# Where the second batch's k and v are averaged: from TensorE's products to VectorE's reductions

## The chip, the cores and the metric

The kernel runs on one core of a Trainium2 chip. The metric is the device time of one execution in microseconds (us); the figure for a kernel is the median of its runs. Five engines work side by side, each through its own queue in order: TensorE (PE in the profile, its weight loads PEld), VectorE (DVE), ScalarE (ACT), GpSimd (POOL) and SyncE (SP), which here issues most DMAs. TensorE writes into PSUM, from where ScalarE and VectorE read.

## The reference, cut to what matters

Attention over pooled keys and values, then a dense feed-forward layer, then a layer of eight experts of which each token takes one. All in float32.

```python
# q, k, v: (8, 8, 576, 64) = batch, head, sequence, head_dim
k_p = k.reshape(B, H, Sp, 8, D).mean(axis=3)        # Sp = 72
v_p = v.reshape(B, H, Sp, 8, D).mean(axis=3)
attn = softmax(q @ k_p.T / sqrt(D))
x = (attn @ v_p) -> (4608, 512)
x = relu(x @ w_in) ** 2 @ w_out                      # d_ff = 2048
out = top-1 of 8 experts: gate * (relu(x @ w1[e]) @ w2[e])
```

The change concerns the first two lines for the second of the eight batches: sums over groups of eight neighbouring rows of k and v.

## The kernel before, in words

The 4608 tokens are 18 tiles of 256: for each batch two "reg" tiles of its first 512 tokens, and after every fourth batch a tile of what is left over. A float32 product is made of three products of split operands (a high part rounded for TensorE, a low part with the rest). One tile against one of eight chunks of the first layer's weights is a step of `Stream.step` (line 352): twelve products for layer 1 (line 285), then ReLU and square on ScalarE and GpSimd (`act_square_first`, line 300), and two steps later six products for layer 2 (`pop`, lines 361 and 336).

The attention of a tile is computed during the tile before it, as small jobs put by hand between those steps. `at(ti, pos, f)` (line 664) files job `f` under tile `ti` and one of 16 positions, two for each chunk; `run_jobs` runs what is filed. The order in which jobs are issued is the order on each engine's queue.

**The first phase.** Tiles 0 and 1 (the first batch) run together, their sixteen steps interleaved by `order` (line 961): tile 0's chunk c sorted at 2c, tile 1's at 2c + 5. Loop index `i` from 0 to 7 runs the jobs filed under tile 0, `i` from 8 to 15 those under tile 1. In the same phase the weights arrive as float64 and have to be converted: `first_steps` (line 250) yields 80 steps, ten for each chunk. Five VectorE instructions join the two 32-bit halves of one half chunk (lines 216 to 229), then ScalarE casts the high part (`wh_m`, line 264) and GpSimd subtracts the low part (`wl_m`, line 265). `conv(n)` issues n such steps. From `i` = 2 to 12 three steps are issued beside a step's layer 1 (`beside`) and three after its layer 2 (`after`), 25 having been issued before. Layer 1 of chunk c needs the first half of its weights, layer 2 the second.

**k and v of a batch.** `pool_load` (line 406) brings k or v into three buffers: two of 128 partitions by 2 x 512 and a third with the rows left over. Each partition holds eight rows of 64 side by side, for one or two heads. `pool_first` (line 437) sums the eight rows of a piece. With a `bank` it lets TensorE add eight products with the identity into a PSUM buffer (lines 448 and 449); with `None` it calls `pool_reduce` (line 433), one VectorE reduction (line 435) that writes into a tile kept in SBUF. Then ScalarE copies the sums twice, each time through a mask that leaves one of the two heads (line 463, tiles `km`, `vb` and `vr`); k's third piece is only copied (line 453, tile `kr`), which a reduction makes unnecessary, as it writes there itself. Batches 2 to 7 use `pool_reduce` and GpSimd.

**The second batch.** Its jobs stand in the first phase. The three pieces of k go to positions 6, 7 and 8 of tile 0 (`plan_k`, list `k` of `FIRST`), which is `i` = 3 and 4; the three of v to positions 0, 1 and 5 of tile 1 (`plan_v`, list `v`), which is `i` = 8, 8 and 10. Around them stands the attention of tile 2 (`plan_reg`, list `tile2`), under tile 1:

- position 0 and 1: the query transposes of the second and the first half (`q_T`, PSUM buffers emptied by ScalarE, line 533), then at position 1 `make_kT`, two groups of transposes of k (lines 489 and 492) that ScalarE copies out (490, 493);
- position 2: scores of the first half and their extremes on VectorE (`scores_first`, lines 561 and 565);
- position 3: the exponentials, eight pairs of ScalarE instructions (line 574);
- position 6: ScalarE's and GpSimd's split of v (`make_vsplit`), normalisation (lines 587 to 595), scores of the second half;
- positions 8 to 15: exponentials and normalisation of the second half, transposes of both (`p_T`, lines 608 and 611), the products with v (`av`, line 624).

All these transposes, scores and sums take turns in one PSUM pool of two buffers, `ps_t` with the tag "tp". A tile that wants a buffer waits until the one before last has been read. `plan_v` files its jobs before `plan_reg` does, so at a shared position v's come first. From tile 2 on tiles run one after the other (line 983). After all 18, the expert phase begins.

Of the kernel before, what the change touches and what calls it, by code (L numbers as in the profile page):

```python
# [25 lines left out]
FIRST = dict(  # L26
    pre=[3, 1, 1, 2, 3, 3], att=[2, 2, 3, 3, 2, 0],
    beside=[0, 0, 3, 3, 3, 3, 3, 3, 3, 3, 3, 3, 3, 0, 0, 0],
    after=[0, 0, 3, 3, 3, 3, 3, 3, 3, 3, 3, 3, 3, 0, 0, 0],
    lag=5, late=11, av=2, spill=[11, 2],  # L30
    k=[6, 7, 8, 11], v=[0, 1, 5, 6, 6], tile2=[1, 0, 1, 2, 3, 6, 6, 8, 9, 10, 13, 15, 15],
    low_dve=[0, 0, 0, 0, 0, 0, 0, 0], bias=[0, 1, 1], vlow_dve=0)


# [8 lines left out]
def moe_pipeline_kernel(  # L43
# [40 lines left out]
    ps_h = ctx.enter_context(tc.tile_pool(name="ps_h", bufs=2, space=bass.MemoryType.PSUM))  # L84
    ps_y = ctx.enter_context(tc.tile_pool(name="ps_y", bufs=2, space=bass.MemoryType.PSUM))
    ps_t = ctx.enter_context(tc.tile_pool(name="ps_t", bufs=2, space=bass.MemoryType.PSUM))
# [319 lines left out]
    def pool_load(src, b, nm):  # L406


        rows = src[b].rearrange("h (a r) d -> (h a) (r d)", r=8).rearrange("(c p) f -> p c f", p=144)
        raws = []  # L410
        for i in range(3):
            raw = akv.tile([P, 2, 512], F32, tag="kvraw", name=f"{nm}raw_{b}_{i}")
            if i < 2:
                nc.sync.dma_start(raw, rows[0:P, 2 * i:2 * i + 2, :])
            elif nm == "k":
                for c in range(4):
                    nc.sync.dma_start(raw[16 * c:16 * c + 16, 0, :], rows[P:144, c, :])
            else:
                pairs = rows[P:144].rearrange("p (g q) f -> p q g f", q=2)
                for j in range(6):  # L420
                    nc.sync.dma_start(raw[16 * j:16 * j + 16], pairs[:, j % 2])
            raws.append(raw)
        return raws

    def pool_dst(nm, b, raws, i):
        if i < 2:
            dst = (kp_t if nm == "k" else vp_t)[b % 2]
            return raws[i], dst[:, 2 * i:2 * i + 2, :]
        if nm == "k":
            return raws[2][:64, 0:1, :], kr_t[b % 2][:, 1:2, :]  # L430
        return raws[2][:96], vr_t[b % 2]

    def pool_reduce(nm, b, raws, i):
        src, dst = pool_dst(nm, b, raws, i)
        nc.vector.tensor_reduce(dst, src.rearrange("p c (r d) -> p c d r", r=8), AX.X, ALU.add)

    def pool_first(nm, b, raws, i, bank):


        src, sums = pool_dst(nm, b, raws, i)  # L440
        n, nc_ = src.shape[0], src.shape[1]
        if bank is None:
            pool_reduce(nm, b, raws, i)
        else:
            src = src.rearrange("p c (r d) -> p c r d", r=8)
            pool, tag, width = bank
            pb_ = pool.tile([P, width], F32, tag=tag, name=f"{nm}sum_{b}_{i}")[:n, 0:nc_ * D]
            for r in range(8):
                nc.tensor.matmul(pb_, ident[:n, :n], src[:, :, r, :], start=r == 0, stop=r == 7)
            sums = pb_.rearrange("p (c d) -> p c d", c=nc_)  # L450
        if nm == "k" and i == 2:
            if bank is not None:
                nc.scalar.copy(kr_t[b % 2][:, 1:2, :], sums)
            return
        if i == 2:
            dst, ms = batch[b].setdefault("vr", a1.tile([96, 2, 2, D], F32, tag="vr", name=f"vr_{b}")), rmask
        else:
            what = "km" if nm == "k" else "vb"
            if what not in batch[b]:
                batch[b][what] = a1.tile([P, 4, 2, D], F32, tag=what, name=f"{what}_{b}")  # L460
            dst, ms = batch[b][what][:, 2 * i:2 * i + 2], mask
        for t in range(2):
            nc.scalar.activation(dst[:, :, t, :], sums, AF.Copy, scale=ms[:n, t:t + 1])
# [14 lines left out]
    def make_km(b, cs=slice(0, 4)):  # L478
        if "km" not in batch[b]:
            batch[b]["km"] = a1.tile([P, 4, 2, D], F32, tag="km", name=f"km_{b}")  # L480
        by_head(batch[b]["km"], kp_t[b % 2], cs)
# [14 lines left out]
    def make_vb(b):  # L496
        if "vb" not in batch[b]:
            batch[b]["vb"] = a1.tile([P, 4, 2, D], F32, tag="vb", name=f"vb_{b}")
            by_head(batch[b]["vb"], vp_t[b % 2], slice(0, 4))
        vr = a1.tile([96, 2, 2, D], F32, tag="vr", name=f"vr_{b}")  # L500
        nc.gpsimd.tensor_tensor(vr, vr_t[b % 2].unsqueeze(2).to_broadcast([96, 2, 2, D]),
                                rmask.unsqueeze(1).unsqueeze(3).to_broadcast([96, 2, 2, D]), ALU.mult)
        batch[b]["vr"] = vr

    def make_vsplit(b, dve, low=True):

        vb, vr = batch[b]["vb"], batch[b]["vr"]
        vh = a3.tile([P, 4, P], F32R, tag="vh", name=f"vh_{b}")
        nc.scalar.copy(vh, vb.rearrange("p c t d -> p c (t d)"))
        nc.scalar.copy(vrem_t[b % 2][:, :, :, D:P], vr)  # L510
        batch[b]["vh"], batch[b]["vrem"] = vh, vrem_t[b % 2]
        if low:
            make_vlow(b, nc.vector if dve else nc.gpsimd)
# [135 lines left out]
        return xh, xl  # L649

    batch = [dict(b=b) for b in range(B)]
    tp_bank, h_bank = (ps_t, "tp", 512), (ps_h, "h", 256)
    xts = {}

    def spill_x(ti):
# [8 lines left out]
    def at(ti, pos, f):  # L664
        jobs.setdefault((ti, pos), []).append(f)

    def plan_k(b):
        m = tiles.index(("reg", b, 0)) - 2
        loc = {}

        def load():
            loc["k"] = pool_load(k, b, "k")
        if b > 1:
            at(m - 1, 13, load)
        else:
            loads[f"k{b}"] = load
        for i in range(3):
            if b < 2:
                at(m, FIRST["k"][i], lambda i=i: pool_first("k", b, loc["k"], i, tp_bank))
            else:  # L680
                at(m, i, lambda i=i: pool_reduce("k", b, loc["k"], i))
        if b > 1:
            at(m, 3, lambda: make_km(b))

    def plan_v(b):
        n = tiles.index(("reg", b, 0))
        loc = {}

        def load():
            loc["v"] = pool_load(v, b, "v")  # L690
        if b > 1:
            at(n - 2, 4, load)
        else:
            loads[f"v{b}"] = load
        for i in range(3):
            if b > 1:
                at(n - 2, (12, 14, 15)[i], lambda i=i: pool_reduce("v", b, loc["v"], i))
            else:
                at(n - 1, FIRST["v"][i], lambda i=i: pool_first("v", b, loc["v"], i, tp_bank))

        tail = tiles[n - 1][0] == "reg" and b % 2 == 0 and b > 0
        if b > 1:
            at(n - 1, 8 if tail else 4, lambda: make_vb(b))
        at(n - 1, 10 if tail else 6 if b > 1 else FIRST["v"][4], lambda: make_vsplit(b, tail))
# [100 lines left out]
    for b in range(B):  # L805
        if b % 2 == 1:
            plan_tail(b - 1)
        if b:
            plan_k(b)
            plan_v(b)  # L810
        plan_reg(b, 0)
        plan_reg(b, 1)
# [232 lines left out]
    def route(ti, ys, yp):  # L1045
        yr = pb2.tile([P, 2, DM + 2], F32, tag="yr", bufs=3, name=f"yr_{ti}")
        lg = pb2.tile([P, 2, NE], F32, tag="lg", name=f"lg_{ti}")
        for u in range(2):
            nc.vector.tensor_tensor(yr[:, u, 0:DM], ys[u], yp[:, u, :], ALU.add)

        def logit(u, e):
            junk = pbr.tile([P, DM], F32, tag="junk", name=f"junk_{ti}_{u}_{e}")
            nc.vector.tensor_tensor_reduce(  # L1053
                out=junk, in0=yr[:, u, 0:DM], in1=wgb[:, e, :], scale=1.0, scalar=0.0,
                op0=ALU.mult, op1=ALU.add, accum_out=lg[:, u, e:e + 1])
        for u in range(2):
            for e in range(NE):
                queue.append(lambda u=u, e=e: logit(u, e))
        st = {}
        fs = [lambda: route_rank(ti, yr, lg, st), None, None, None, lambda: route_count(ti, st),  # L1060
              lambda: route_place(ti, yr, st), None, None, lambda: route_scatter(0, st),
              lambda: route_store(ti, yr), *[None] * SCATTER_GAP, lambda: route_scatter(1, st)]
        if ti == TA:
            fs += after_a()
        if ti == NT - 1:
            fs += after_b()
        queue.append(lambda: chain(fs))
# [402 lines left out]
    for i_, (what, g) in enumerate(items):  # L1470
# [7 lines left out]
        i, c = divmod(g, NCH)  # L1478
# [4 lines left out]
        if g < N1:  # L1483
            x = xb[i]
            stream.step(wch_b[c], x, act_square_b, c, state, f"b{i}_{c}",
                        lambda ys, i=i: route(i, ys, ypb[i]), side)
# [44 lines left out]
```

## Time and profile before

| | |
|---|---|
| median of 3 runs | 1552.11 us (1548.74 to 1552.5) |
| the profiled execution | 1552.05 us |
| its span, first to last instruction | 1550.2 us |
| TensorE busy | 1502.2 us (97%) |
| TensorE's weight loads busy | 1355.9 us (87%) |
| VectorE busy | 1115.5 us (72%) |
| ScalarE busy | 677.5 us (44%) |
| GpSimd busy | 417.2 us (27%) |
| mean granted TensorE clock | 0.979 of full speed |

Times inside the profile count from the first instruction. "Busy" leaves out waits. The time of a group is the sum of its instructions; "idle before" is the time for which the engine had stood still when an instruction began, with the instruction of another engine that ended the wait behind an arrow. Products on TensorE overlap, so their recorded times add up to more than the time that passes. A float32 product with the identity has two records.

### The profile page before, as it was taken

How to read it: one execution, taken by the hardware profiler on the slowest of the kernel's cores; microseconds unless marked ns; L12 is line 12 of the kernel's file. 1: busy time of each engine (PE TensorE's matmuls, PEld its weight loads, DVE VectorE, ACT ScalarE, POOL GpSimd, SP SyncE). 2: the span in 40 equal slices, each digit the busy share in tenths (PEclk: the TensorE clock that was granted, in tenths of full speed). 3: DMA queues.
4: the chain of work that ended last, by engine and by line, in shares of the span. 5: the costliest groups of instructions: out<-in, count | busy, mean ns of one | idle time of the engine just before them, and what ended most of it. 6: DMA issues, size and time to landing. Idle time of an engine off the chain costs nothing. (4 is left out here: it accounts for less than half of the span.)

```text
span 1550.2 us, 27286 instructions
## 1 busy us (share of the span) xinstructions
PE 1502.2 (97%) x9678; PEld 1355.9 (87%) x9678; DVE 1115.5 (72%) x2349; ACT 677.5 (44%) x1422; POOL 417.2 (27%) x506
## 2 busy tenths in 40 slices
PE   6799999999999999999999999999999999999997
PEld 5688889898989999999999999989989888888886
DVE  7776797689867554477777778789866767767763
ACT  4453333233333323444344343355555656665663
POOL 3253335353534434010110111131222221222211
PEclk8699999999999999999999999999999999999999
DMA  9314355446623314655677667599877878888862
GB/s 297 114 56 143 112 167 180 134 159 159 179 86 95 98 57 163 211 96 87 104 98 95 76 103 96 103 213 202 242 256 215 262 255 272 260 265 254 268 226 89
DMA packets 214343, 253.75 MB, mean 164 GB/s; under 512 B 56959, under 2 KB 139007, under 8 KB 214080
## 3 DMA queue, kind: packets, MB, share of 16 engines
q1 hardware_dynamic: 202784, 221.73, 52.3%
q0 software_dynamic: 11424, 30.28, 8.9%
q8 instruction: 76, 1.25, 0.4%
q14 instruction: 59, 0.48, 0.1%
HBM read 198.00 MB, written 55.80 MB: 164 GB/s over the span
## 5 line engine op out<-in xcount | busy, mean ns | idle before, releaser
L1053 DVE CUSTOM_DVE_ANT_0 junk<-yr,wgb 128x512 f32<-128x512 f32 x288 | 198.0, 688 | 4.7
L192 DVE TENSOR_TENSOR wl_s<-raw_s,wh_s 128x1024 fp32r<-128x1024 f32 x144 | 174.8, 1222 | 28.8 <-ACT wh_s L191 26.4
L285 PE MATMUL h_a<-xh,wh_m 128*128 128x256 f32 x576 | 151.2, 294 | 5.2 <-ACT wh_m L264 5.0
L191 ACT CAST wh_s<-raw_s 128x1024 fp32r<-128x1024 f32 x144 | 149.1, 1046 | 10.1 <-DMA raw_s<-in_moe_w_dram 10.1
L285 PE MATMUL h_a<-xl,wh_m 128*128 128x256 f32 x576 | 148.0, 288 | 1.6 <-DVE xl L635 1.6
L316 ACT ACTIVATE r_b<-h_b 128x256 f32<-128x256 f32 x144 | 55.3, 384 | 212.8 <-PE h_b L285 208.9
L285 PE MATMUL h_s<-xh_s,wh_s 128*128 128x256 f32 x576 | 145.6, 286 | 2.2 <-DVE gl_s L326 2.2
L285 PE MATMUL h_b<-xh_b,wh_f 128*128 128x256 f32 x576 | 144.8, 284 | 0.0
L285 PE MATMUL h_b<-xl_b,wh_f 128*128 128x256 f32 x576 | 144.2, 283 | 0.0
L285 PE MATMUL h_s<-xl_s,wh_s 128*128 128x256 f32 x576 | 143.6, 282 | 0.0
L294 ACT ACTIVATE r_a<-h_a 128x256 f32<-128x256 f32 x128 | 49.2, 385 | 212.9 <-PE h_a L285 142.7
L296 POOL TENSOR_TENSOR g_a<-r_a 128x256 f32<-128x256 f32 x128 | 83.0, 648 | 183.3 <-ACT r_a L294 182.9
L1124 POOL DMA_INDIRECT perm_d<-pos,di x36 | 38.2, 1060 | 347.9 <-DVE es L1115 177.8
L319 DVE TENSOR_TENSOR gl_b<-g_b,gh_b 128x256 fp32r<-128x256 f32 x144 | 61.2, 425 | 95.8 <-ACT g_b L318 95.8
L297 POOL TENSOR_TENSOR gl_a<-g_a,gh_a 128x256 fp32r<-128x256 f32 x128 | 96.7, 756 | 102.3 <-DVE gh_a L295 56.5
L336 PE MATMUL y_a<-wh_m,gh_a 128*128 128x512 f32 x288 | 121.7, 423 | 0.0
L285 PEld LDWEIGHTS h_a<-xh,wh_m 128*128 128x128 f32 x576 | 111.9, 194 | 10.1 <-ACT wh_m L264 5.6
L1317 POOL DMA_INDIRECT out_dram<-yo,tidx x36 | 42.0, 1166 | 284.2 <-ACT yo L1314 198.2
L285 PEld LDWEIGHTS h_a<-xl,wh_m 128*128 128x128 f32 x576 | 112.1, 195 | 6.8 <-DVE xl L635 3.3
L336 PE MATMUL y_a<-wl_m,gh_a 128*128 128x512 f32 x288 | 116.5, 405 | 0.0
L285 PEld LDWEIGHTS h_s<-xh_s,wh_s 128*128 128x128 f32 x576 | 108.9, 189 | 8.5 <-DVE gl_s L326 3.7
L336 PE MATMUL y_a<-wh_m,gl_a 128*128 128x512 f32 x288 | 115.9, 402 | 0.0
(322 smaller groups left out, 4144.9 us busy)
## 6 DMA issues: line engine op xcount, KB each, us to landing
raw_s<-in_moe_w_dram SPq DMA_DIRECT2D x288, 256.0 KB, 4.2
raw_h<-in_moe_w_dram SPq DMA_DIRECT2D x112, 256.0 KB, 4.0
y_d<-yr POOLq DMA_DIRECT2D x18, 514.0 KB, 10.2
xs_d<-xh SPq DMA_DIRECT2D x18, 512.0 KB, 2.7
xs_d<-xl SPq DMA_DIRECT2D x18, 512.0 KB, 4.0
yp_d<-ya SPq DMA_DIRECT2D x36, 256.0 KB, 2.1
xh_b<-xs_d SPq DMA_DIRECT2D x18, 512.0 KB, 9.3
xl_b<-xs_d SPq DMA_DIRECT2D x18, 512.0 KB, 11.5
```

The lines of the kernel that those rows point to most:

```text
L191: nc.scalar.copy(wh, raw)
L192: nc.vector.tensor_tensor(wl, raw, wh.bitcast(F32), ALU.subtract)
L285: nc.tensor.matmul(h, w_[:, 0, kk * P:(kk + 1) * P], rhs[:, kk, :], start=n == 0, stop=n == 3 * NK - 1)
L294: nc.scalar.activation(r, h, AF.Relu)
L296: nc.gpsimd.tensor_tensor(g, r, r, ALU.mult)
L297: nc.gpsimd.tensor_tensor(gl, g, gh.bitcast(F32), ALU.subtract)
L316: nc.scalar.activation(r, h, AF.Relu)
L319: nc.vector.tensor_tensor(gl, g, gh.bitcast(F32), ALU.subtract)
L336: nc.tensor.matmul(ys[u], lhs[:, ts], rhs[:, 1, :], start=(c == 0 and n == 0), stop=(c == NCH - 1 and n == 2))
L1053: nc.vector.tensor_tensor_reduce(out=junk, in0=yr[:, u, 0:DM], in1=wgb[:, e, :], scale=1.0, scalar=0.0, op0=ALU.mult, op1=ALU.add, accum_o ...
L1124: nc.gpsimd.indirect_dma_start(out=perm_d[:, :], out_offset=bass.IndirectOffsetOnAxis(ap=st["di"][:, u:u + 1], axis=0), in_=st["pos"][:, u ...
L1317: nc.gpsimd.indirect_dma_start(out=out[:, :], out_offset=bass.IndirectOffsetOnAxis(ap=ti_[:, u:u + 1], axis=0), in_=yo[:, :], in_offset=No ...
```

## The change

For the second batch, `pool_first` is called without a bank, for k and for v. So the six sums are VectorE reductions into SBUF tiles, and ScalarE's masked copies read those instead of PSUM; for k's third piece the copy falls away. The third piece of v moves from position 5 of tile 1 to position 3, where the exponentials of tile 2's first half are filed too. The first batch is left as it was.

```diff
-    k=[6, 7, 8, 11], v=[0, 1, 5, 6, 6], tile2=[1, 0, 1, 2, 3, 6, 6, 8, 9, 10, 13, 15, 15],
+    k=[6, 7, 8, 11], v=[0, 1, 3, 6, 6], tile2=[1, 0, 1, 2, 3, 6, 6, 8, 9, 10, 13, 15, 15],
...
-    tp_bank, h_bank = (ps_t, "tp", 512), (ps_h, "h", 256)
+    h_bank = (ps_h, "h", 256)
...
-                at(m, FIRST["k"][i], lambda i=i: pool_first("k", b, loc["k"], i, tp_bank))
+                at(m, FIRST["k"][i], lambda i=i: pool_first("k", b, loc["k"], i, None))
...
-                at(n - 1, FIRST["v"][i], lambda i=i: pool_first("v", b, loc["v"], i, tp_bank))
+                at(n - 1, FIRST["v"][i], lambda i=i: pool_first("v", b, loc["v"], i, None))
```

## Rows read from the trace of the kernel before

**Rows 1.** Stretches: length, busy PE, PEld, DVE, ACT, POOL; PEclk, DMA share, GB/s.

```profile
59.30:95.31 36.01, 32.06 (x190) 28.37 (x189) 35.09 (x46) 14.32 (x37) 17.56 (x15) 0.81 0.40 118
88.00:114.00 26.00, 25.72 (x184) 23.67 (x183) 18.17 (x26) 16.53 (x55) 14.43 (x12) 1.00 0.00 1
126.40:800.00 673.60, 667.22 (x4453) 608.97 (x4452) 481.73 (x1022) 228.23 (x529) 222.17 (x300) 0.99 0.49 129
800.00:1550.00 750.00, 737.44 (x4644) 659.30 (x4642) 543.27 (x1188) 387.53 (x694) 147.94 (x147) 1.00 0.75 196
```

**Rows 2.** TensorE in order of time, 78 to 116 us (start, duration, instruction).

```profile
78.83 0.39 PE L285 MATMUL h_a<-xh,wh_m 128*128 128x256 f32 x1 [1.74 <-ACT wh_m L264]
...
94.64 1.95 PE L449 MATMUL vsum<-vraw,ident 128*128 128x128 f32 x16
...
97.89 0.27 PE L492 MATMUL pk<-ident,kr 64*128 64x64 f32 x1
...
115.31 0.66 PE L608 MATMUL pp<-ident,p 128*128 128x128 f32 x4 [0.53 <-ACT p L574]
```

**Rows 3.** VectorE in order of time, 74 to 104 us.

```profile
74.48 0.69 DVE L229 SCALAR_TENSOR_TENSOR t<-raw,t 128x512 f32<-128x512 int32 x1
...
89.13 0.69 DVE L225 SCALAR_TENSOR_TENSOR t<-raw,t 128x512 int32<-128x512 int32 x1
...
92.42 0.69 DVE L219 SCALAR_TENSOR_TENSOR t<-raw,t 128x512 int32<-128x512 int32 x1
...
100.31 0.95 DVE L565 TENSOR_REDUCE mx<-sc 128x4 f32<-128x288 f32 x2 [4.99 <-PE sc L561]
...
103.79 0.43 DVE L222 TENSOR_SCALAR raw<-raw 128x512 int32<-128x512 int32 x1
```

**Rows 4.** The sums by products, line 449, 55 to 115 us; ns min/median/max.

```profile
L449 PE MATMUL ksum<-kraw,ident x48: 270/275/366, 61.3 to 71.9; 128*128 128x128 f32 x32, 64*64 64x64 f32 x16
...
L449 PE MATMUL vsum<-vraw,ident x48: 270/275/275, 91.0 to 106.5; 128*128 128x128 f32 x32, 96*96 96x128 f32 x16
```

**Rows 5.** VectorE's reductions, line 435, whole span; ns min/median/max.

```profile
L435 DVE TENSOR_REDUCE kp<-kraw x13: 1872/1981/2006, 4.6 to 479.1; 128x128 f32<-128x1024 f32 x13
L435 DVE TENSOR_REDUCE vp<-vraw x12: 1948/1976/2025, 152.6 to 503.4; 128x128 f32<-128x1024 f32 x12
L435 DVE TENSOR_REDUCE kr<-kraw x7: 1018/1043/1061, 7.5 to 482.8; 64x64 f32<-64x512 f32 x7
L435 DVE TENSOR_REDUCE vr<-vraw x6: 1919/1980/1991, 160.1 to 505.3; 96x128 f32<-96x1024 f32 x6
```

**Rows 6.** ScalarE in order of time, 78 to 112 us.

```profile
78.18 0.60 ACT L264 CAST wh_m<-t 128x512 fp32r<-128x512 f32 x1
...
97.14 0.60 ACT L533 ACTIVATE qT<-pq 128x512 f32<-128x512 f32 x1
...
101.37 0.31 ACT L574 ACTIVATE p<-sc,mx 128x72 f32<-128x72 f32 x1
...
105.57 0.62 ACT L264 CAST wh_m<-t 128x512 fp32r<-128x512 f32 x1 [0.64 <-DVE t L229]
106.76 0.62 ACT L463 ACTIVATE vr<-vsum,rmask 96x128 f32<-96x128 f32 x2 [0.57 <-PE vsum L449]
108.20 0.39 ACT L305 ACTIVATE r_a<-h_a 128x256 f32<-128x256 f32 x1 [0.82 <-PE h_a L285]
...
109.93 0.62 ACT L264 CAST wh_m<-t 128x512 fp32r<-128x512 f32 x1 [0.59 <-DVE t L229]
...
111.28 0.20 ACT L587 ACTIVATE sm<-sm 128x8 f32<-128x8 f32 x1
```

**Rows 7.** SyncE's queue: the last loads of the second batch's v.

```profile
72.23 2.68 SPq L421 DMA_DIRECT2D vraw<-in_v_dram  x6
```

**Rows 8.** Two short stretches, columns as in Rows 1.

```profile
76.00:80.00 4.00, 2.26 (x16) 1.97 (x15) 3.86 (x7) 1.62 (x4) 1.65 (x2) 0.93 1.02 405
80.00:86.00 6.00, 5.39 (x15) 4.32 (x15) 5.89 (x7) 2.13 (x5) 3.47 (x4) 0.50 0.84 186
```

## The prediction, written before the changed kernel was timed

> **What bounds the kernel now.** I read the page's busy shares first, then stretches of the span, then the order of single instructions on each engine around the change. After 126.4 us TensorE does nearly everything: it is busy 667.22 of 673.60 us and then 737.44 of 750 us [rows 1]. A delay that has reached TensorE by then is carried to the end almost one to one, so only what happens before 126.4 us has to be worked out. In that early part another engine sets the pace. From 59.30 to 95.31 us VectorE is busy 35.09 of 36.01 us, nearly all of it with the five-step joins of the first weights, while TensorE waits for what the joins feed, as at 78.83 us [rows 1, 2]. The change takes work from TensorE, partly where it waits, and gives it to VectorE where it has no gap; VectorE's first real gap is the 4.99 us before its instruction at 100.31 us [rows 3].
>
> **What is removed.** Six groups of eight products leave TensorE, 96 records in all [rows 4]; a group of 16 records takes 1.95 us [rows 2], so at most 11.7 us. The small copy of ScalarE for the third piece of k goes too; it lies in an idle moment and I cost it at nothing. The PSUM buffers that the sums used are no longer taken.
>
> **What is added.** Six reductions on VectorE of kinds that the trace already has. 128x1024 to 128x128 takes 1.98 us, 64x512 takes 1.04, 96x1024 takes 1.98 [rows 5]. For k that is 1.98 + 1.98 + 1.04 = 5.0 us, for v 3 x 1.98 = 5.9 us. ScalarE's masked copies stay, but their input now comes from VectorE, and whatever stands behind them in ScalarE's queue waits with them.
>
> The reduction's price is where the Trainium skill differs from the row. The trace has 1.98 us for 1024 elements per partition, and no full-size one under 1.87 [rows 5]. In "VectorE: DVE Perf Modes", sections "Specifications" and "The perf-mode tier table", tensor_reduce has only the mode of one element per cycle, at 0.96 GHz: an estimate of 1.07 us. By that figure k would cost VectorE 2.7 us, and steps 1 to 4 below would end at +2.6 us instead of +6.6. The measured row decides.
>
> **Step 1, k (up to 88 us).** The three reductions stand between join steps that run without a gap. The first half of the fifth chunk is joined at 74.48 + 0.69 = 75.17 us [rows 3]; behind all three reductions at 80.17. Its cast on ScalarE then starts at 80.2 instead of 78.18 us [rows 6], and TensorE goes on at 80.8 instead of 78.83 [rows 2]: 2.0 us late. The removed k products lie ahead of its waits for such casts, so they return nothing there. SyncE's queue holds v's loads until k's buffers are read; the last six leave at 72.23 us now [rows 7] and up to 5 us later afterwards. v is first wanted at 94.8 us, so that costs nothing; the stores and query loads behind them are for tile 2 and later, and I cost them at nothing too.
>
> **Step 2, v's first two pieces (88 to 98 us).** The join step ahead of the first piece ends at 89.13 + 0.69 = 89.82 us [rows 3]; with k's 5.0 it ends at 94.8, and the reduction at 96.8. Three join steps follow, which end at 92.42 + 0.69 = 93.11 now, 3.29 us after: so 100.1, and the second reduction ends at 102.1. One relief: join steps beside GpSimd's work are stretched. Unstretched they take 0.69 or 0.43 us [rows 3], a half of three long and two short ones 2.93, and 45 steps 26.4 us; so 8.7 of the 35.09 us are stretch, for 15 GpSimd instructions in 36 us [rows 1]. The reductions hardly vary [rows 5], so a GpSimd instruction beside one stretches nothing: the 8.96 us of five reductions meet some 3.7 of them, a relief of 2.2 us at most and of nothing at least. I take 1.0, so 101.1.
>
> Now the queues. ScalarE makes the two masked copies of the second piece (0.62 us, as those at 106.76) and only then empties the transposed queries (0.60) [rows 6]. TensorE's small transpose of k at 97.89 us [rows 2] needs the PSUM buffer of those queries, as there are two such buffers. So it starts at 101.1 + 0.62 + 0.60 = 102.3 us, **4.4 us late**. TensorE itself, two groups of products lighter, would be there at 97.89 + 2.0 - 3.9 = 96.0 us. It waits over 6 us, with ready layer-1 products behind the transpose in its queue.
>
> **Step 3, v's third piece, brought forward.** The scores and their maximum follow 4.4 us late: VectorE's 100.31 becomes 104.7. VectorE itself is there at 95.32 + 8.96 - 1.0 = 103.3, so of its gap of 4.99 us 1.4 is left. From the maximum to the end of three more join steps are 103.79 + 0.43 - 100.31 = 3.91 us [rows 3]: 108.6. There the third reduction now stands: 110.6. Its two masked copies (0.62) go ahead of the exponentials in the same job slot, so the exponentials start at 111.2 instead of 101.37 us [rows 6]: **9.8 us late**. 5.4 of it comes from the new place of that piece: 2.8 for join steps for which the exponentials did not wait before, 2.0 and 0.6 for the piece.
>
> **Step 4, what ScalarE has to spare.** From 101.37 to 111.28 us ScalarE idles 0.64 + 0.57 + 0.82 + 0.59 = 2.6 us and makes those 0.62 us of copies [rows 6]. Both go, so it is 9.8 - 3.2 = 6.6 us late at 111.28. Then come the second exponentials, and TensorE waits for them at 115.31 us already today [rows 2]. So TensorE takes over the 6.6 us there.
>
> **TensorE's clock.** After the gap of 1.74 us before 78.83 us the granted clock was 0.93 from 76 to 80 and 0.50 (1.2 of 2.4 GHz) from 80 to 86, though TensorE was busy 5.39 of those 6 us [rows 8]. The change opens one gap of 6 us, and shorter ones up to 125 us. A low stretch where TensorE waits anyway costs little; one like that at 80 to 86 us in the saturated part costs half its length, 3 us, and two cost 6. I bound it by 0 and 6 and take 2, nearest to one stretch partly hidden in waits.
>
> **Sum.** 6.6 + 2 = +8.6 us. The profiled execution took 1552.05 us, beside a median of 1552.11: I forecast **1561**. With the full relief of 2.2 us and no clock loss it is +5.4 (1557); with no relief and the 6 us it is +13.6 (1566).
>
> **Rivals.**
> *Absorbed.* The reductions cover so much of GpSimd's work that k's 5.0 us are gone by 88 us. Then v's second piece ends at 93.11 + 3.96 = 97.1, the transpose starts 0.4 us late, but the exponentials still stand behind the third piece: 100.31 + 0.4 + 3.91 + 1.98 + 0.62 = 107.2, 5.8 us late, and 2.6 after the spare: 1554.7, or 1552 if later gaps take the rest. For it: 8.7 us of stretch. Against: only 2.2 of it meets reductions. In the Trainium skill, "SBUF — State Buffer", section "Who interferes with whom", speaks for it: on trn2 tensor_reduce never contends with GpSimd. The even durations agree [rows 5]. What the other page's rate gave above also lands here. Chance 0.20.
>
> *Faster: TensorE was the bound.* Between 88 and 114 us it is busy 25.72 of 26 us [rows 1]. If the gap of 4.99 us takes v's first two pieces (3.96), k costs nothing, and the third piece is ready before the exponentials, v's products return 3 x 1.95 = 5.9 us: 1546.2. It decides at 97.89 us: ScalarE must have emptied the queries before TensorE asks. For it: the full TensorE. Against: ScalarE's order, and the wait at 115.31 us, where an earlier TensorE only waits longer. Chance 0.08.
>
> *Worse.* More than two low-clock stretches in the saturated part: above 1566. Chance 0.05.
>
> That the change would not do what it says I see no room for: the branch without a bank exists, and batch 0 runs it.
>
> **How the numbers follow.** The forecast (1557 to 1566) has the remaining 0.67. The range reaches down into the absorbed case, to 1553. About 0.3% (4.7 us) is what a measurement of this kernel can tell from no change. Slower by more: the forecast and the worse case, less 0.02 for a forecast in which all terms come low, 0.70. The same: the absorbed case and that 0.02, 0.22. Faster: 0.08.
>
> **What would show it.** Right: the reduction line has 38 + 6 instructions, the product line loses 96 records, the small transpose of k waits some 4 to 6 us for ScalarE, the first exponentials of tile 2 start near 111 us, and tile 2's first layer 1 begins near 135 instead of 126.4 us. Step 1 is wrong if TensorE's start behind the fifth chunk's cast isn't 1 to 2 us later; step 2 if the transpose doesn't wait; step 3 if the exponentials start before 106 us. The forecast falls if tile 2 begins before 131 us.

## The result, and the profile after

The changed kernel takes **1563.37 us** (median of 4 runs, 1561.86 to 1564.91) beside 1551.18 of the kernel before in the same runs (4 runs): ratio 1.008, 95% interval 1.0063 to 1.0098. The forecast was 1561, range 1553 to 1566. The profiled execution took 1563.52 us, its span is 1561.7 us (before 1550.2), its mean granted clock 0.974 (before 0.979).

TensorE's busy time fell from 1502.2 to 1496.4 us and VectorE's rose from 1115.5 to 1123.5: the work moved as intended, and the kernel became slower. The two lines that did the sums, in the profile after:

```profile
L435 DVE TENSOR_REDUCE kp<-kraw x15: 1858/1971/2022, 4.7 to 486.0; 128x128 f32<-128x1024 f32 x15
L435 DVE TENSOR_REDUCE vp<-vraw x14: 1858/1978/2016, 95.0 to 510.3; 128x128 f32<-128x1024 f32 x14
L435 DVE TENSOR_REDUCE kr<-kraw x8: 1020/1042/1058, 7.6 to 489.7; 64x64 f32<-64x512 f32 x8
L435 DVE TENSOR_REDUCE vr<-vraw x7: 1921/1980/2000, 109.2 to 512.2; 96x128 f32<-96x1024 f32 x7
...
L449 PE MATMUL vsum<-vraw,ident x32: 273/275/275, 14.4 to 17.8; 128*128 128x128 f32 x32
...
L449 PE MATMUL ksum<-kraw,ident x16: 274/421/553, 6.5 to 9.8; 128*128 128x128 f32 x16
```

Six reductions more than in [rows 5], at the same price; the two groups of 48 records of [rows 4] are gone, and what is left of that line is the first batch's, before 18 us.

The stretches of [rows 1] in the profile after, with the same columns:

```profile
59.30:95.31 36.01, 24.03 (x124) 20.86 (x123) 35.29 (x44) 12.93 (x32) 16.32 (x14) 0.83 0.39 118
88.00:114.00 26.00, 16.82 (x96) 14.63 (x94) 21.92 (x28) 10.40 (x37) 7.98 (x7) 0.80 0.00 1
126.40:800.00 673.60, 667.78 (x4449) 609.53 (x4448) 478.46 (x1008) 230.01 (x533) 223.19 (x302) 0.98 0.48 131
800.00:1550.00 750.00, 746.05 (x4693) 667.81 (x4692) 549.29 (x1206) 390.72 (x703) 153.85 (x146) 1.00 0.74 196
```

From 88 to 114 us TensorE was busy 25.72 us before and is busy 16.82 now, and the granted clock fell from 1.00 to 0.80. VectorE was full up to 95 us and still is. Behind 126 us TensorE is busy nearly all the time in both.

TensorE in order of time, after (start, duration, instruction, wait before it and what ended it):

```profile
79.64 0.38 PE L285 MATMUL h_a<-xh,wh_m 128*128 128x256 f32 x1 [3.23 <-ACT wh_m L264]
...
98.13 1.11 PE L489 MATMUL pk<-ident,km 128*128 128x128 f32 x4 [5.36 <-ACT qT L533]
101.61 0.37 PE L492 MATMUL pk<-ident,kr 64*128 64x64 f32 x1 [2.36 <-ACT qT L533]
...
122.73 0.66 PE L608 MATMUL pp<-ident,p 128*128 128x128 f32 x4 [1.73 <-ACT p L574]
...
133.82 0.28 PE L285 MATMUL h_a<-xh,wh_m 128*128 128x256 f32 x1
...
1026.89 1.04 PE L1291 MATMUL px<-ident,xg 128*128 128x128 f32 x4 [3.21 <-DMA xg<-y_d,pidx]
```

Against [rows 2] the first row is 0.81 us late, the small transpose of k (L492) 3.72, the transposes of the first p 7.42. The row at 133.82 is tile 2's first layer 1, at 126.40 before: 7.42 late. The last row is the first product on the rows that the experts gather; there the delay grows by another 3 us. ScalarE in order of time, after, shows why the waits for qT and p are there:

```profile
78.97 0.62 ACT L264 CAST wh_m<-t 128x512 fp32r<-128x512 f32 x1 [1.38 <-DVE t L229]
...
100.38 0.69 ACT L463 ACTIVATE vb<-vp,mask 128x128 f32<-128x128 f32 x2 [1.79 <-DVE vp L435]
100.98 0.57 ACT L533 ACTIVATE qT<-pq 128x512 f32<-128x512 f32 x1
...
111.20 0.69 ACT L463 ACTIVATE vr<-vr,rmask 96x128 f32<-96x128 f32 x2 [4.69 <-DVE vr L435]
111.80 0.30 ACT L574 ACTIVATE p<-sc,mx 128x72 f32<-128x72 f32 x1
...
118.11 0.20 ACT L587 ACTIVATE sm<-sm 128x8 f32<-128x8 f32 x1
```

Each time a masked copy of v waits for VectorE (1.79, 4.69 us), and the work that TensorE wants, qT and the exponentials, stands right behind it. VectorE, after:

```profile
77.72 1.22 DVE L229 SCALAR_TENSOR_TENSOR t<-raw,t 128x512 f32<-128x512 int32 x1
...
98.45 1.90 DVE L435 TENSOR_REDUCE vp<-vraw 128x128 f32<-128x1024 f32 x1
...
105.68 0.95 DVE L565 TENSOR_REDUCE mx<-sc 128x4 f32<-128x288 f32 x2 [3.67 <-PE sc L561]
...
109.19 1.98 DVE L435 TENSOR_REDUCE vr<-vraw 96x128 f32<-96x1024 f32 x1
```

### The profile page after: what moved, and what is told of

Its sections match the earlier page's. It is cut to its first block, busy times and chain, and to the rows that moved or that the text cites. A ratio compares the mean times of both kernels' runs of the same rounds, so it can differ in the third digit from the quotient of the medians.

```text
span 1561.7 us, 27090 instructions
## 1 busy us (share of the span) xinstructions
PE 1496.4 (96%) x9582; PEld 1349.6 (86%) x9582; DVE 1123.5 (72%) x2355; ACT 677.3 (43%) x1421; POOL 421.9 (27%) x506
## 5 line engine op out<-in xcount | busy, mean ns | idle before, releaser
L1124 POOL DMA_INDIRECT perm_d<-pos,di x36 | 41.6, 1155 | 351.8 <-DVE es L1115 174.4
## 6 DMA issues: line engine op xcount, KB each, us to landing
y_d<-yr POOLq DMA_DIRECT2D x18, 514.0 KB, 10.1
xl_b<-xs_d SPq DMA_DIRECT2D x18, 512.0 KB, 11.5
```

Source lines behind the costliest of these rows:

```text
L1124: nc.gpsimd.indirect_dma_start(out=perm_d[:, :], out_offset=bass.IndirectOffsetOnAxis(ap=st["di"][:, u:u + 1], axis=0), in_=st["pos"][:, u ...
```

## The experiments

**How far two executions of one kernel lie apart.** *b_again* is the kernel before, unedited.

> The kernel before, once more, to see how far one profiled execution stands from another. The first phase has no data-dependent waits, so tile 2's first layer 1 begins at 126.4 us within 0.5. What differs between two executions of the same kernel after that is scatter: if it is 2 us or more, then the 4.1 us by which the changed kernel loses further ground after tile 2 (7.4 us late at 133.8 us, 11.5 at the end) may be scatter too. Time: ratio 1.000 within 0.2%.

1549.80 us (1547.95 to 1557.27, 10 runs), ratio 1.000 [0.9987, 1.0013]. The time agrees; the landmark (the start of one named instruction) doesn't: tile 2 begins at 123.05 us, 3.35 earlier than in the first profile of the same program. The two part at 70 us. One stretch with the columns of [rows 1], in the kernel before and then in *b_again*:

```profile
70.00:76.00 6.00, 6.00 (x30) 5.08 (x30) 5.83 (x9) 1.82 (x5) 2.34 (x2) 0.50 0.25 73
```

```profile
70.00:76.00 6.00, 4.31 (x36) 3.64 (x35) 5.83 (x9) 3.34 (x9) 3.09 (x3) 1.00 0.44 145
```

At a granted clock of 0.50 TensorE needs all six microseconds for 30 records, at 1.00 it does 36 in 4.31. ScalarE's next work waits for it, and the cast of [rows 6] at 78.18 us comes at 75.43. So one profile fixes tile 2's start to no better than 3.4 us, and what follows leans on waits inside a profile and on several profiles. Counted from the start of VectorE's first join instruction (59.3 to 60.2 us in these five profiles), tile 2 begins 67.1 and 63.5 us later in the two profiles of the kernel before, and 74.2, 76.0 and 75.9 later in three of the changed kernel (two come below): means 65.3 and 75.4, **10 us** of loss ahead of tile 2.

**One half at a time.** *k_only* sums k on VectorE and leaves v with TensorE at its old places; *v_only* is the reverse, with v at positions 0, 1, 3.

```
k_only: FIRST v=[0, 1, 5, 6, 6];  pool_first("v", ..., tp_bank)
v_only: pool_first("k", ..., tp_bank)
```

> Only k's sums on VectorE, v as before. Theory (one gap, two claims): VectorE's gap of 4.99 us before the maximum at 100.31 us takes k's 5.0 us whole, and TensorE makes good the 2 us of step 1 by the products it no longer has; tile 2 begins at 126.4 to 127.4 us, ratio 1.000 to 1.001. Rival (every us on VectorE costs its share): 5.0 of 10.9 us, so 3.4 of the 7.4 us: tile 2 at 129.8, ratio 1.002 to 1.003. Rival (k carries the loss, as the part without any gap): +5 us or more.

> Only v's sums on VectorE, third piece at position 3, k as before. Theory: the small transpose of k waits little (VectorE is 5.0 us earlier than in the changed kernel), but the exponentials still stand behind the third piece's reduction; they start 5 to 7 us late and tile 2 begins 3 to 5 us late, at 129.5 to 131.5; ratio 1.002 to 1.004. Rival (shares): 4.0 us, the same; told apart by k_only. Rival (TensorE was the bound): tile 2 begins earlier than 126.4, as 5.3 us of products are gone.

k alone: 1553.26 us (1551.57 to 1553.99, 10 runs), 1.0016 [1.0007, 1.0026], tile 2 at 126.17. That is a time between its theory's and its first rival's. v alone: 1560.47 (1559.92 to 1562.57, 4 runs), 1.0068 [1.0049, 1.0086], tile 2 at 131.76. That is a larger loss than the 1.002 to 1.004 expected. VectorE's added work is nearly the same, 5.0 and 5.9 us, and the cost 2.9 and 10.1 us beside the kernel before of the same runs (1550.33). So the cost is not a matter of VectorE's time alone. In *v_only* ScalarE waits as it does after:

```profile
107.58 0.70 ACT L463 ACTIVATE vr<-vr,rmask 96x128 f32<-96x128 f32 x2 [4.94 <-DVE vr L435]
108.19 0.30 ACT L574 ACTIVATE p<-sc,mx 128x72 f32<-128x72 f32 x1
```

The exponentials began at 101.37 us in [rows 6]; with v alone they begin at 108.19, though k's transpose is on time beside that profile (97.74 and 97.89, both with a clock of 0.50 from 70 to 76 us).

**Where k's 5 us went.** *k_twice* is *k_only* with each reduction of k issued twice.

```
+            if b == 1:
+                pool_reduce(nm, b, raws, i)
             pool_reduce(nm, b, raws, i)
```

> The kernel with k alone on VectorE, with each of k's three reductions issued twice (the second to the same place; the result is the same), so VectorE has 5.0 us more ahead of 90 us. Theory (VectorE's single gap of 4.99 us ahead of the first maximum took k's 5.0 us; there is no second one): the second 5.0 us are paid, 3 to 5 us at the beginning of tile 2 and 3 to 5 us of time: 1556.5 to 1558.5 beside 1553.3 for k alone. Rival (k is nearly free because TensorE's removed products give back what VectorE takes, or because reductions cover GpSimd's work): the added reductions go the same way, time within 1.5 us of k alone, 1552 to 1555.

VectorE's first maximum, with the wait before it, in *k_only* and then in *k_twice*:

```profile
100.08 0.95 DVE L565 TENSOR_REDUCE mx<-sc 128x4 f32<-128x288 f32 x2 [0.45 <-PE sc L561]
```

```profile
104.15 0.95 DVE L567 TENSOR_REDUCE mx<-sc 128x4 f32<-128x288 f32 x2 [0.45 <-PE sc L563]
```

In [rows 3] the same instruction came at 100.31 with 4.99 us of idle time before it. Beside that profile k's sums filled the gap down to 0.45 and moved nothing; the next 5 us found none and moved the maximum by 4.07 us and tile 2 by 4.09 (126.17 to 130.26). That is the theory's size. But the gap belongs to that one execution. In *b_again*, the same kernel without the low clock from 70 to 76 us, the instruction is:

```profile
96.98 0.95 DVE L565 TENSOR_REDUCE mx<-sc 128x4 f32<-128x288 f32 x2 [0.45 <-PE sc L561]
```

There VectorE has 0.45 us to spare and not 4.99, and beside it k's first 5 us move the maximum by 3.1 us and tile 2 by 3.12. The 2.9 us that *k_only* loses in time are nearer to this. So k's sums cost tile 2 nothing or 3 us, by the execution that one compares with.

The time of *k_twice* isn't the theory's (1.0058 [1.0042, 1.0074]): the profiled execution took 1555.77, 0.7 us below the expected 1556.5 to 1558.5, but 8 of the 10 runs lie between 1560.8 and 1566.56 (median 1563.48, before 1553.18). What cost those some 6 us more no profile shows; it stays open.

**The third piece's place.** *a_v5* is the changed kernel with v's third piece back at position 5.

```
-    v=[0, 1, 3, 6, 6]
+    v=[0, 1, 5, 6, 6]
```

> The changed kernel with v's third piece back at position 5. By step 3 and 4 of the prediction its place costs 5.4 us at the exponentials, of which 3.2 are spare: tile 2 would begin 2.2 us earlier than in the changed kernel, at 131.6, and the time would be some 2 us lower. Rival (ScalarE's queue only shifts the wait): the exponentials start 5 us earlier, near 106.5, but ScalarE's copies of the third piece then wait for VectorE behind the casts, and the normalisation at position 6 is as late as it was: tile 2 at 133.5 to 134.5, no gain.

1562.35 us (1562.23 to 1566.5, 4 runs), 1.0084 [1.0062, 1.0106]: no gain. The first exponentials do come early, at 106.35, 5.45 us earlier than after; the prediction had put 5.4 on the place. But ScalarE's queue holds the same wait again, one job further on:

```profile
116.08 0.70 ACT L463 ACTIVATE vr<-vr,rmask 96x128 f32<-96x128 f32 x2 [4.89 <-DVE vr L435]
116.68 0.36 ACT L305 ACTIVATE r_a<-h_a 128x256 f32<-128x256 f32 x1
...
118.74 0.40 ACT L510 CAST vrem<-vr 96x256 fp32r<-96x256 f32 x1
119.04 0.20 ACT L587 ACTIVATE sm<-sm 128x8 f32<-128x8 f32 x1
```

The first exponentials' sums (L587) stand behind it, and VectorE's second maximum waits for those: 120.38, beside 119.87 after. TensorE's transposes of p start at 123.23, beside 122.73. Tile 2 begins later than either expectation had it, by the clock:

```profile
124.00:128.00 4.00, 3.90 (x13) 2.97 (x12) 1.28 (x3) 2.79 (x11) 0.74 (x1) 0.50 0.00 0
```

```profile
136.39 0.28 PE L285 MATMUL h_a<-xh,wh_m 128*128 128x256 f32 x1
```

After a wait of 4.46 us for p the granted clock (third from the end of the first row) was 0.50, and TensorE took 13.16 us from the transposes of p to tile 2; after, with a clock of 1.00 there, it took 11.09 (122.73 to 133.82).

**ScalarE's order alone.** *copies_late* keeps the reductions where the change put them and moves ScalarE's masked copies of v to position 4, behind qT and the exponentials. With "sums" `pool_first` makes the reduction alone, with "copies" the masked copies alone. It ran twice, each time beside the changed kernel unedited (*a_again*, *a_third*).

```
-at(n - 1, FIRST["v"][i], lambda i=i: pool_first("v", b, loc["v"], i, None))
+at(n - 1, FIRST["v"][i], lambda i=i: pool_first("v", b, loc["v"], i, "sums"))
+at(n - 1, 4, lambda i=i: pool_first("v", b, loc["v"], i, "copies"))
```

> The changed kernel with one edit: the reductions of v stay on VectorE at positions 0, 1 and 3 of tile 1, but ScalarE's masked copies of all three pieces move to position 4, behind the emptying of the transposed queries and behind tile 2's exponentials. Work is the same on every engine; only ScalarE's queue is in another order. Theory (ScalarE's queue passes the wait for VectorE on to TensorE): the small transpose of k comes 1 to 2 us earlier than in the changed kernel (101.6 us), at some 100; the first exponentials start right behind the maximum, near 107 instead of 111.8 us; tile 2 begins 3 to 4 us earlier than 133.8, at 130 to 131; time 1559 to 1561 beside 1563.4. Rival (what costs is VectorE's added time itself, in whatever order ScalarE stands): tile 2 begins within 1.5 us of 133.8 and the time stays at 1562 to 1565. The two executions of the unchanged kernel lay 3.35 us apart at that point, so the medians decide, not one profile.

> The changed kernel with v's masked copies at position 4 of tile 1 once more, as the four times of its first run did not tell it from the changed kernel. Theory (ScalarE's queue passes VectorE's lateness on): tile 2 begins at 130 to 132 us, and the median is 2 to 4 us below the changed kernel's of the same call. Rival (VectorE's time alone sets it): tile 2 within 1.5 us of the changed kernel's, medians within 1 us of each other.

In *copies_late_5*, first ScalarE, then TensorE:

```profile
97.71 0.62 ACT L264 CAST wh_m<-t 128x512 fp32r<-128x512 f32 x1 [3.84 <-DVE t L229]
98.24 0.59 ACT L537 ACTIVATE qT<-pq 128x512 f32<-128x512 f32 x1
...
103.70 0.31 ACT L578 ACTIVATE p<-sc,mx 128x72 f32<-128x72 f32 x1
```

```profile
98.88 0.37 PE L496 MATMUL pk<-ident,kr 64*128 64x64 f32 x1 [4.30 <-ACT qT L537]
...
119.33 0.66 PE L612 MATMUL pp<-ident,p 128*128 128x128 f32 x4 [3.27 <-ACT p L578]
...
131.94 0.28 PE L285 MATMUL h_a<-xh,wh_m 128*128 128x256 f32 x1
```

With no other work and no less of it, k's transpose comes 2.7 us earlier than after, the exponentials 8.1, p's transposes 3.4; tile 2 begins 71.2 and 72.1 us after the first join beside 74.2 to 76.0. At the landmarks the theory holds (tile 2 at 131.34 and 131.94, about where it was expected), and its rival (within 1.5 us) falls. But the new order takes away 3.7 of the 10 us ahead of tile 2, and 6.4 stay (71.7 on average, beside 65.3 in the kernel before). ScalarE still stands for VectorE ahead of qT, now 3.84 us at the cast of a join. So the masked copies are one way by which VectorE's added work reaches TensorE, and not the only one; no run tells the others apart. Nor do the times follow: 1564.36 (4 runs) beside 1567.14 of *a_again* (1561.82 to 1568.33, 5 runs), and 1562.56 (6 runs) beside 1560.75 of *a_third* (1560.04 to 1567.53, 5 runs). Both pairs scatter by over 5 us, so 3.7 us at tile 2 were not shown to reach the end.

**The unedited partners.**

> The changed kernel once more, unedited, for the scatter between two executions. Theory (a clock scatter ahead of tile 2, and a scatter of TensorE's wait for the first gather of the experts): tile 2 begins at 133.8 within 3.5 us, and the wait for the first gathered rows is anything from 0.3 to 3.2 us. Rival (that wait comes from the change): it is 3 us or more again. Median 1562 to 1565 by both.

> The changed kernel, unedited, as the partner of copies_late_5 on the same chip. Theory and rival agree: ratio to the kernel before 1.007 to 1.009, tile 2 begins 133.5 to 136.5 us. Where TensorE's wait for the first gathered rows of the experts belongs to the program, it is 3.2 to 3.4 us for a third time; where it is scatter, it is anywhere from 0.3 to 3.4.

Ratios 1.0071 [1.0049, 1.0093] and 1.0066 [1.0051, 1.008]: the loss repeats. TensorE's wait for the first gathered rows is 3.39 and 3.41 us, after 3.21 in the first profile. It belongs to the program, as the rival of *a_again* had it. Tile 2 begins at 136.20 and 135.70 us, 1.9 to 2.4 later than in the first profile. Of that, 1.4 and 1.5 us lie between the transposes of p and tile 2 (12.47 and 12.63 us beside 11.09), where the clock was low behind the wait of 1.73 us for p. The stretch in *a_again*, clock 0.57 (after 1.00):

```profile
124.00:128.00 4.00, 3.44 (x13) 2.62 (x12) 0.96 (x2) 2.87 (x13) 0.25 (x1) 0.57 0.00 0
```

**v on VectorE, but late.** *v_late_t2* and *v_late_5* are one kernel: k's sums on TensorE, v's on VectorE at positions 0, 1, 9, tile 2's jobs ahead of them. *t2_only* has the same places with v on TensorE.

```
v=[0, 1, 9, 6, 10], tile2=[0, 0, 0, 1, 1, 4, 4, 5, 9, 9, 12, 14, 14]
```

> A kernel meant to beat both: k as in the kernel before (TensorE's products); v's pieces on VectorE at positions 0, 1 and 9 of tile 1, the split at 10, and tile 2's jobs pulled ahead (0, 0, 0, 1, 1, 4, 4, 5, 9, 9, 12, 14, 14), so that the queries, k's transposes, scores and exponentials no longer stand behind v's masked copies of the second and third piece on ScalarE. Theory (the loss came from the order of the queues, not from VectorE's 5.9 us): 3 to 7 us faster than the kernel before, 1544 to 1548, with tile 2 beginning at 118 to 123 us. Rival (VectorE's time is paid wherever the reductions stand, or the earlier jobs wait for tile 1's queries and joins themselves): 1551 or more.

> The kernel before with the positions of v_late_t2 (v at 0, 1, 9, split at 10, tile 2's jobs at 0, 0, 0, 1, 1, 4, 4, 5, 9, 9, 12, 14, 14), but v still summed by TensorE: nothing of the change is in it. Theory (the earlier positions alone bring tile 2 forward; v on VectorE late adds little either way): tile 2 begins at 120 to 125 us, time within 3 us of the kernel before. Rival (v's products on TensorE are what fills that stretch, and VectorE's sums at late positions save them): tile 2 begins 4 to 6 us later than v_late_t2's 121.6. On the wait for the first gathered rows: if it is a matter of VectorE's added reductions, it is under 0.5 us here as in two runs of the kernel before; if any shift of the order ahead of tile 2 brings it, it is 1.3 us or more.

> v_late_t2 once more, beside t2_only on the same chip, as its ten times ran from 1551.9 to 1562.7. Theory (VectorE's time is free where the queues behind it are: positions late in tile 1): median within 2 us of the kernel before or faster, tile 2 at 120 to 123 us, so that some 8 us of the change's loss are the places and not the engine. Rival (its first median, 2.9 us above the kernel before, is real): ratio 1.001 to 1.004 again, with tile 2 early and the time lost behind it, at the experts' start, by a wait of 2 us or more for the first gathered rows.

TensorE in *v_late_5*, and tile 2's first layer 1 in *t2_only*:

```profile
94.31 0.27 PE L492 MATMUL pk<-ident,kr 64*128 64x64 f32 x1
...
121.50 0.28 PE L285 MATMUL h_a<-xh,wh_m 128*128 128x256 f32 x1
```

```profile
127.61 0.28 PE L285 MATMUL h_a<-xh,wh_m 128*128 128x256 f32 x1
```

Both profiles have the clock of the kernel before (0.50 from 70 to 76 us and 0.51 from 80 to 86, beside 0.50 and, in [rows 8], 0.50), so they compare well: tile 2 begins **6.1 us** earlier, and three groups of v's products are 3 x 1.95 = 5.9 us [rows 2]. In size, the move gives back ahead of tile 2 what it takes from TensorE; it is the rival "faster" of the prediction, in other places of the queues. *t2_only* missed its expected 120 to 125, as its rival had said: the places alone gain nothing (1553.25 us, 1.0013 [1.0, 1.0025]). As a whole neither kernel beats the one before, and the 1544 to 1548 us expected of *v_late_t2* did not come: 1556.07 (10 runs), 1.0021 [0.9998, 1.0044], and again 1552.74 (1545.93 to 1556.96, 11 runs), 1.0011 [1.0, 1.0023]. The 1545.93 is the profiled execution itself. So the early tile 2 is shown for two executions (121.64 and 121.50), not for the median. Beside *v_only* (1.0068) the same 5.9 us on VectorE cost less in these places. Much of the scatter lies behind the landmarks: from TensorE's first product on gathered rows to the end of the span one profile of this kernel takes 538.1 us and the other 534.1.

**What comes back at the experts.** In every profile with added reductions TensorE waits for the first gathered rows: 1.33 us (*a_v5*), 1.57 and 2.24 (v late), 1.76 (*k_only*), 2.31 (*k_twice*), 2.37 (*v_only*), 2.68 and 2.89 (copies late), 3.21 to 3.41 (the changed kernel). In the three profiles without (before and *b_again*, which are one program, and *t2_only*) it is 0.24, 0.39 and none. GpSimd's scatter ahead of that gather, in *b_again* and then after:

```profile
995.08 1.02 POOL L1124 DMA_INDIRECT perm_d<-pos,di  x1 [3.65 <-DMA pidx<-perm_d]
```

```profile
1006.54 1.02 POOL L1124 DMA_INDIRECT perm_d<-pos,di  x1 [4.43 <-DMA pidx<-perm_d]
```

The small index load ahead of it lands 0.8 us later. That is a part of the 2.8 us by which TensorE's wait is longer; the other 2.0 arise behind the scatter (18.3 us from it to TensorE's first product on gathered rows in *b_again*, 20.35 after). At the moment of the index load SyncE sends off six loads of experts' weights. In each of the three profiles without added reductions one of the six took long to issue (1.04 us before, 0.78 in *b_again*, 1.21 in *t2_only*), so the rest followed later; in the eleven profiles with them all take 0.35 to 0.42. The third load, in *b_again* and then after:

```profile
990.32 0.78 SPq L184 DMA_DIRECT2D raw_s<-in_moe_w_dram  x1
```

```profile
1001.00 0.38 SPq L184 DMA_DIRECT2D raw_s<-in_moe_w_dram  x1
```

That weight loads crowd the gather's index is what these rows suggest. No run changed the loads' order, and why one issue is slow in those three profiles isn't known: argued, not shown.

## Why the prediction was right, and where it wasn't

The direction and the time hold, and so does the mechanism in the main: v's masked copies wait for VectorE in ScalarE's queue, ahead of qT and the exponentials. That they wait there the rows show; what this order costs *copies_late* puts at 3.7 of 10 us ahead of tile 2. The steps below are measured beside the first profile of the kernel before, from which the prediction counted. In *b_again* the same landmarks stand 2.7 to 3.4 us earlier, so the agreement of single steps to within a us is partly luck. By steps:

- **Step 1, k.** Wrong in size and in its footing. VectorE's join ends at 77.72 + 1.22 = 78.94 us, forecast 80.17: the reductions covered more of GpSimd's work than allowed (two of k's three had some of it beside them, at their usual 1.97 and 1.06 us). TensorE's start behind the cast is 0.81 us late, below the 1 us that the prediction had set as its own mark. And the 78.83 us that it counted from were themselves late, by the low clock from 70 to 76 us; beside *b_again* (76.11) the same start is 3.5 us late. The gap of 4.99 us, on which the prediction built too, is 0.45 there. So k's price at tile 2 is nothing beside the one profile and 3.1 us beside the other, and 2.9 us in time. Of the rival "absorbed", k's part held beside the first profile only; v's didn't hold.
- **Step 2, v's first two.** Right for the small transpose: 101.61, forecast 102.3. But its own wait is 2.36 us and not 4 to 6; 5.36 us come one job earlier, where the large transposes wait for the qT behind v's first piece, which the step did not have. v's second reduction ends at 100.35, forecast 101.1. The relief taken as 1.0 us was thus 1.75 by this row, near its upper bound of 2.2.
- **Step 3, the third piece.** Exponentials at 111.80, forecast 111.2. The 0.6 came from the clock: 0.50 from 101 to 105 us, so the way from the small transpose to the maximum took 4.07 us (101.61 to 105.68) instead of 2.42 (97.89 to 100.31), which made up for the larger relief. That 5.4 us belong to the piece's place is right for the exponentials (5.45 in *a_v5*) and wrong as a price: the piece back in its place gives none of it back.
- **Step 4, ScalarE's spare.** Forecast 6.6 us at the first sums (L587) and at TensorE's transposes of p; measured 6.83 (118.11 beside 111.28) and 7.42.
- **The clock, +2.** In the first profile no low stretch fell into a full TensorE; the low one lies where TensorE works off a wait, and cost 1.65 us on the chain to the maximum. In the two other profiles of the changed kernel, *a_again* and *a_third*, one did, and cost 1.4 and 1.5 us ahead of tile 2. So the term was of the right kind and size in two profiles of three.
- **The sum, +8.6.** The median rose by 12.2 us, the span of the profiled execution by 11.5: 7.4 by tile 2, 3 at the experts' start, some 1 between. Beside *b_again* the span rose by 13.7: 10.8 by tile 2, 2.8 at the experts' start. So the terms ahead of tile 2 may be too small as well, if the second profile is the usual one. The term that is missing beside both is that of the experts' start, which no step had: the prediction let a delay be carried "to the end almost one to one" [rows 1], but a chain of DMAs ahead of the first gather doesn't keep step with TensorE.
- **The rival "faster"** fell for this change (*v_only* frees the 5.9 us and loses 10); *v_late_5* shows places in which it comes true as far as tile 2, though not in the time. **"Worse"** didn't happen in the first four runs; the five of *a_again* have a median of 1567.14, beside 1553.18 of the kernel before.
- **A side sum.** For a reduction of 1.07 us the prediction ends at +2.6 us. That leaves out its relief of 1.0 us; with a relief in proportion it is +2.0. The forecast doesn't rest on it.

## What to carry to other kernels

Five or six microseconds on a full engine cost some two to three us here, or ten, by what stands behind them (*k_only* and v late, *v_only*). Find the engine's next gap, in more than one profile, and then the queue of the engine that takes the result, because an in-order queue hands one late input to all that follows. Moving the late instruction back by a job only helps if nobody stands behind it there. And compare landmarks over several profiles: here one program put the same instruction 3.35 us apart.

## What had not been expected of the hardware

- Two executions of one program stand 3.35 us apart at 123 us of the span, with a granted clock of 0.50 or 1.00 from 70 to 76 us, while their spans differ by 0.15% (1550.2 and 1547.9 us).
- Issuing a weight load took SyncE 0.78 to 1.21 us once in each of three profiles (of two programs), and 0.35 to 0.42 in the eleven others; TensorE's wait for a gather some 24 us later was 0.4 us or less in the three and 1.33 to 3.41 in the eleven.
- The loss of clock behind a short wait is not the same in every execution: behind the same wait of 1.73 us TensorE kept 1.00 in one profile of the changed kernel and fell to 0.57 from 124 to 128 us in two others.
